# Loading v as nine consecutive tokens per partition, with its quadrants moved on VectorE and the left-over keys of two heads taken together

## The chip, the cores and the metric

The kernel runs on one core of a Trainium2 chip. The time is the device time of one execution in microseconds (us); it is given as the median of several runs. Five engines run side by side, each with its own instruction list in order: TensorE (PE in the profile; PEld is its weight load), VectorE (DVE), ScalarE (ACT), GpSimd (POOL) and SyncE (SP). They wait for one another by semaphores. 16 DMA engines move data between the chip's memory (HBM) and the on-chip memory (SBUF); PE writes its results to PSUM, which DVE and ACT read.

## The reference

Two stages, cut to what matters. First an attention over 8 batches, 8 heads, 576 tokens and 64 channels, with a bias from the running sum of a gate s:

```python
scores = q @ k.T / sqrt(64)
cum = cumsum(max(s, 0))
bias = -(cum[query] - cum[key])
scores = where(key > query, -1e9, scores + min(bias, 0))
x = softmax(scores) @ v                  # [8, 576, 8*64]
```

Then a mixing of the lowest 64 frequencies of x along the tokens, with one complex 512x512 matrix per frequency, and a product with w_ch:

```python
X = rfft(x, axis=tokens)[:64]
Y = X @ (w_r + 1j * w_i)                 # per frequency
u = x + irfft(Y, n=576)
out = u + max(u @ w_ch, 0)               # [8, 576, 512] float32
```

The 64 pairs of matrices are 134 MB in float32; q, k and v are 9.4 MB each.

## The kernel before

**Steps.** The attention goes in 32 steps n. Step n handles batch b = n % 8 of head pair g = n // 8, so both heads of a pair. The order of work is written out by hand: the loop near the end of the attention part calls, in each step, `load` (issues DMAs on POOL), `cum_rows` (the queries' part of the bias, by SP), `scores(n, 0)`, `av(n-1, 1)`, `mode_products(n)`, `transposes(n+1, 0)`, `scores(n, 1)`, `transposes(n+1, 1)`, `fft(n-1)` and `av(n, 0)`. PE, DVE and ACT each run their own instructions in the order of these calls. In steps 26 to 31 two products with w_ch for rows that are already complete are put in: `first_transposed(i, 0)` after `scores(n, 1)`, and `first_product(i, 0)`, `first_transposed(i, 1)`, `first_product(i, 1)` after `av(n, 0)`. `first_transposed` is four transposes on PE and a copy by DVE (xt, L538); `first_product` is four matmuls (z_ps, L546) on that copy.

**q and k** are loaded by `loads_qk` for two steps at once, 18 consecutive tokens per partition, turned by PE (tr_ps, L340) in two halves and copied to qt and kt, three of four copies by DVE and one by ACT (L344).

**Scores.** Keys are taken in two windows of 256 tokens, W = 2*P, and each window in two tiles r of 128 keys: tile r holds the keys 2p + r of partition p. `scores(n, h)` makes, for r = 0 and 1, one PSUM tile `sc_ps` of 1,024 columns from a pool of two buffers (`scpool`): two matmuls that write the causal mask (negm, L376), three that add the scores of both windows (L382), and two exps on ACT that write p_sb in fp16 (L390), 576 and 320 queries wide. The last 64 tokens of the 576 are left over; their keys come from `scores4`, called for both heads together with the second head's first tile: it writes 64 spare columns of that same PSUM tile (L353, L357), for the last 64 queries alone, and one exp makes p4 (L361).

**v** is loaded by `loads_v` in each step, one DMA per head with 2 consecutive tokens per partition (512 bytes in memory, 256 as fp16), straight into the layout that `av` reads (v2, five buffers); the 64 left-over tokens of all batches of a head pair come by `loads_tails` in two DMAs into v4.

**av(n, h)** multiplies p by v for five blocks of 128 queries: 17 matmuls with 65 columns (64 channels and a one, which gives the softmax's sum; L418). The sums of the two tiles r lie in two columns, so DVE adds them (den, L423), inverts (L427) and scales the result into x_all (L428).

**fft and modes.** `fft(n-1)` transforms x_all (L443) and DVE copies the result to xs in four casts (L453). `modes(g, c)` multiplies xs by the weights of eight frequencies (L463); the products for head pair g are made while pair g+1 is in the attention, those of the last pair after step 31.

**Loads.** All loads of q, k, v and weights are issued by POOL (L234) in the order of the lists given to `load`, which spreads the lists over one another; each issue waits for one of eight semaphores taken in turn, so for the DMA eight issues before, and, where a buffer is used again, for its reader. Weights have a ring of 11 and one of 6 buffers and eight early places; the memory types are changed from float32 to 16 bits by the DMA.

**After step 31** come the mode products of the last head pair, one group of eight frequencies after another as their weights arrive, with products with w_ch between them, and then the output, 18 DMAs.

Of the kernel before, what the change touches and what calls it, by code (L numbers as in the profile page):

```python
# [18 lines left out]
def kernel(  # L19
# [11 lines left out]
    nc = tc.nc  # L31
# [23 lines left out]
    W = 2 * P  # L55
    NWN = S // W
    NK = 2 * NWN
    HM = NM // 2
# [3 lines left out]
    ident_np = np.eye(P, dtype=np.float32)  # L62
    negm_np = np.concatenate(
        [np.where(2 * np.arange(P)[:, None] + r > np.arange(W)[None, :], -1.0e9, 0.0) for r in range(2)],
        axis=1,
    )
    nat = np.arange(NL)
    negm4_np = np.concatenate([np.where(nat[:, None] > nat[None, :], -1.0e9, 0.0)] * 2, axis=0)
# [55 lines left out]
    NV = LA + 2  # L124
    VW = 66


    v2 = [ap_.tile([P, 2 * NWN * W + P], FP16, name=f"v2_{i}") for i in range(NV)]

    v4 = [ap_.tile([P, B, VW], FP16, name=f"v4_{i}") for i in range(2)]  # L130
    NP_ = 3
    poff = [0]
    for w in range(NWN):
        for r in range(2):
            poff.append(poff[-1] + SP - w * W)
    p_sb = [ap_.tile([P, poff[-1]], FP16, name=f"p_sb{i}") for i in range(NP_)]
    p4 = [ap_.tile([P, P], FP16, name=f"p4_{i}") for i in range(2)]

    temp = xs_flat[1].bitcast(FP32)
    ident32, negm32, s_sb = temp[:, :P], temp[:, P : P + 2 * W + NL], temp[:NPAIR, -S:]  # L140
    ident16 = ap_.tile([P, P], BF16, name="ident16")
    negm = ap_.tile([P, 2 * W + NL], BF16, name="negm")
# [20 lines left out]

    def loads_v(n):

        if n >= N:
            return []
        g, b = divmod(n, B)
        return [
            (  # L170
                v2[n % NV][:, : 2 * NWN * W].rearrange("p (w h c) -> p w h c", w=NWN, h=2)[:, :, h, P:],
                v[b, 2 * g + h, : NF * P, :].rearrange("(w p r) d -> p w (r d)", p=P, r=2),
            )
            for h in range(2)
        ]

    def loads_tails(g):

        if g >= NG:
            return []  # L180
        return [
            (
                v4[g % 2][NL * h : NL * h + NL, :, :D],
                v[:, 2 * g + h, NF * P :, :].rearrange("b t d -> t b d"),
            )
            for h in range(2)
        ]


# [75 lines left out]
    load(loads_w(W0), loads_v(0) + loads_tails(0) + first[2:] + loads_v(1))  # L265
# [7 lines left out]
    with tc.tile_pool(name="cum_psum", bufs=1, space=PSUM) as cpsum:  # L273
        spos = s_sb
        zer, cum = (p_sb[i][:NPAIR, :].bitcast(FP32)[:, :S] for i in (0, 1))
# [9 lines left out]
        keys = cum[:, : NF * P].rearrange("c (w p r) -> c w r p", p=P, r=2)  # L285
        for x in range(NK):
            nc.tensor.transpose(
                ct_ps[:, x, :], keys[:, x // 2, x % 2, :], ident32[:NPAIR, :NPAIR]
            )

        tl = p_sb[2][:NPAIR, :].bitcast(FP32)[:, : 2 * NL].rearrange("p (x t) -> p x t", x=2)
        for x in range(2):
            nc.vector.tensor_copy(out=tl[:, x, :], in_=cum[:, (NT - 1) * P :])
        nc.tensor.transpose(
            ct_ps[:, NK, :], tl.rearrange("p x t -> p (x t)"), ident32[:NPAIR, :NPAIR]
        )
        nc.vector.tensor_copy(out=cumt_sb, in_=ct_ps)
        for x in range(2):
            rows = slice(NL * x, NL * x + NL)
            nc.vector.tensor_copy(  # L300
                out=cumt4[rows, :], in_=cumt_sb[rows, NK, x::2]
            )
# [4 lines left out]
    for i in range(NV):  # L307
        for c in (P - 1, W):
            nc.vector.memset(
                v2[i][:, c : c + (2 * NWN - 1) * W + 1 : W], 1.0  # L310
            )
    for i in range(2):
        nc.vector.memset(v4[i][:, :, D : D + 1], 1.0)
        nc.vector.memset(p4[i][:, NL * (1 - i) : NL * (2 - i)], float(1 - i))
# [17 lines left out]
    def transposes(n, half):  # L332
# [8 lines left out]
        for i, dst in enumerate((qt, kt)):  # L341
            copy = (nc.vector.tensor_copy, nc.scalar.copy)[half * i]
            to = dst[n % NQ][:D].rearrange("d h (p r) -> d h p r", r=R)
            copy(  # L344
# [629 lines left out]
```

## Time and profile before

| what | value |
|---|---|
| median of 3 runs | 443.83 us (443.63 to 443.93) |
| span of the profiled execution | 441.4 us; the median of the runs is 2.4 us above it |
| busy, share of the span | PE 344.0 us (78%), DVE 253.2 (57%), ACT 226.2 (51%), POOL 241.5 (55%) |
| DMA | 93.25 MB in 72,768 packets, 29,760 of them under 512 B |
| v loads | 72 DMAs of 64 KB, 0.72 us of POOL each |
| weight loads | 256 KB each, median 8.5 to 9.1 us from issue to landing |
| start of step 8, 16, 24, 26, 31 (L357 on PE) | 75.0, 151.1, 243.8, 276.6, 326.6 us |
| first mode product after step 31 | 335.6 us |
| last weights used | 405.4 to 407.5 us |

How to read it: the page cuts the span in 40 slices of 11 us; a digit is the busy share in tenths, for DMA the mean of its 16 engines. A line of a timeline is: start in us, length in us, engine, line of the kernel, operation, what it writes <- what it reads, shape, count; in brackets the idle time of the engine just before it and what ended that. Sizes in GB/s are counted on the written side, so 16-bit data that come from float32 count half of what is read.

### The profile page before, as it was taken

The numbers are of one execution on the slowest core, as the hardware profiler recorded it, in microseconds if no ns is written. First come the engines' busy times: TensorE is split into PE (matmuls) and PEld (weight loads), VectorE is DVE, ScalarE is ACT, GpSimd is POOL, SyncE is SP. The second block draws the span as 40 slices with busy tenths as digits, with TensorE's granted clock in tenths as the row PEclk, the third lists the DMA queues.
The fourth block names the chain that finished last, engine by engine and source line by source line (L and its number), as shares of the span: only waits on it lengthen the run. The fifth ranks groups of instructions, "written<-read, shape, count | busy, mean of one in ns | idle before, by whom it ended". The sixth has DMA issues, their size and how long they took to land.

```text
span 441.4 us, 10806 instructions
## 1 busy us (share of the span) xinstructions
PE 344.0 (78%) x4409; PEld 207.5 (47%) x4409; DVE 253.2 (57%) x574; ACT 226.2 (51%) x421; POOL 241.5 (55%) x381
## 2 busy tenths in 40 slices
PE   1688998898686978792956658989987887787994
PEld 1455656465354545460634325655554445442341
DVE  7766775676545546471643515766655443451795
ACT  1486788267545725571543324666650424420794
POOL 7766566565565655555655555555544444440293
PEclk9998999999969889896786967999998988998999
DMA  9999999999999999999999999999999999998498
GB/s 180 201 206 206 204 206 205 207 207 206 209 199 207 205 208 207 207 207 208 202 206 206 208 207 203 208 205 206 200 209 211 209 210 209 210 213 163 154 383 343
DMA packets 72768, 93.25 MB, mean 211 GB/s; under 512 B 29760, under 2 KB 31296, under 8 KB 72720
## 3 DMA queue, kind: packets, MB, share of 16 engines
q0 software_dynamic: 63408, 81.29, 105.0%
q1 hardware_dynamic: 9312, 11.29, 7.7%
q8 instruction: 34, 0.56, 0.5%
q14 instruction: 14, 0.11, 0.1%
HBM read 163.51 MB, written 9.44 MB: 392 GB/s over the span
## 4 chain that ended last, share of the span: by engine, by line
DMA 53%; PE 24%; DVE 12%; issue 5%; ACT 3%; POOL 2%; DVEq 0%; ACTq 0%; POOLq 0%
DMA w_sb<-in_moe_w_i_dram 31%; DMA w_sb<-in_moe_w_r_dram 20%; PE yp L463 3%; PE sc_ps L382 3%; PE z_ps L655 3%; DMA qk<-in_k_dram 2%; PE u_ps L781 2%; DVE qt L344 2%; PE sc_ps L376 2%; POOL w_sb L234 2%; PE u_ps L751 2%; DVE xs L453 2%; PE av_ps L418 2%; PE tr_ps L340 2%; DVE xt L538 1%
## 5 line engine op out<-in xcount | busy, mean ns | idle before, releaser
L390 ACT ACTIVATE p_sb<-sc_ps,cumt_sb 128x576 f16<-128x576 f32 (+1 forms) x256 | 141.9, 636 | 22.2 <-PE sc_ps L382 21.8
L234 POOL DMA_DIRECT2D w_sb<-in_moe_w_r_dram x120 | 71.1, 594 | 59.1 <-DMA w_sb<-in_moe_w_i_dram 18.1
L234 POOL DMA_DIRECT2D w_sb<-in_moe_w_i_dram x120 | 70.9, 593 | 55.0 <-DMA w_sb<-in_moe_w_i_dram 20.2
L382 PE MATMUL sc_ps<-qt,kt 128*128 128x512 bf16 (+2 forms) x384 | 78.3, 317 | 8.2 <-ACT kt L344 7.5
L344 DVE COPY qt<-tr_ps 64x576 bf16<-64x576 bf16 x64 | 47.8, 746 | 52.5 <-PE tr_ps L340 52.5
L234 POOL DMA_DIRECT2D v<-in_v_dram x72 | 52.0, 722 | 41.3 <-DMA w_sb<-in_moe_w_r_dram 10.7
L340 PE MATMUL tr_ps<-ident,qk 64*64 64x64 bf16 x1152 | 34.6, 205 | 43.9 <-DMA qk<-in_k_dram 15.0
L382 PEld LDWEIGHTS <-kt 128*128 128x128 bf16 x384 | 38.7, 106 | 37.2 <-ACT kt L344 14.7
L340 PEld LDWEIGHTS <-qk 64*64 64x64 bf16 x1152 | 26.5, 117 | 60.7 <-DVE kt L344 19.0
L376 PE MATMUL sc_ps<-negm,ident 128*128 128x256 bf16 x256 | 54.2, 297 | 0.2
L463 PE MATMUL yp<-w_sb,xs 128*32 128x512 bf16 (+1 forms) x480 | 42.0, 415 | 15.2 <-DMA w_sb<-in_moe_w_i_dram 13.6
L361 ACT ACTIVATE p<-sc_ps,cumt 128x64 f16<-128x64 f32 x32 | 10.1, 314 | 78.0 <-PE sc_ps L357 77.8
L418 PE MATMUL av_ps<-v,p_sb 128*128 128x65 f16 x1024 | 44.3, 197 | 1.2 <-DVE x_all L428 0.5
L344 ACT COPY kt<-tr_ps 64x576 bf16<-64x576 bf16 x32 | 22.9, 715 | 37.7 <-DVE qt L344 37.2
L418 PEld LDWEIGHTS <-p_sb 128*128 128x128 f16 x1024 | 37.8, 100 | 8.4 <-DVE x_all L428 3.4
L453 DVE CAST xs<-ft_ps 64x128 bf16<-64x128 f32 x128 | 36.6, 286 | 7.2 <-PE ft_ps L443 5.8
L423 DVE TENSOR_REDUCE den<-av_ps 128x5 f32<-128x10 f32 x64 | 10.8, 169 | 50.3 <-PE av_ps L418 49.3
L463 PEld LDWEIGHTS <-xs 128*32 128x32 bf16 (+1 forms) x512 | 18.9, 145 | 32.2 <-DMA w_sb<-in_moe_w_i_dram 14.0
L428 DVE TENSOR_TENSOR x_all<-av_ps,rcp 128x320 f16<-128x320 f32 x64 | 31.5, 492 | 2.2
L524 ACT COPY z<-z_ps 128x512 f32<-128x512 f32 x22 | 12.9, 586 | 26.7 <-PE z_ps L546 14.1
L443 PE MATMUL ft_ps<-Ff_sb,x_all 128*64 128x192 f16 (+1 forms) x320 | 24.1, 264 | 1.0 <-DVE x_all L428 1.0
L344 DVE COPY kt<-tr_ps 64x576 bf16<-64x576 bf16 x32 | 24.4, 762 | 0.4
(108 smaller groups left out, 432.9 us busy)
## 6 DMA issues: line engine op xcount, KB each, us to landing
w_sb<-in_moe_w_r_dram POOLq DMA_DIRECT2D x120, 256.0 KB, 8.5
w_sb<-in_moe_w_i_dram POOLq DMA_DIRECT2D x117, 256.0 KB, 9.1
out_dram<-r_w SPq DMA_DIRECT2D x16, 512.0 KB, 3.0
v<-in_v_dram POOLq DMA_DIRECT2D x72, 64.0 KB, 7.4
qk<-in_q_dram POOLq DMA_DIRECT2D x15, 288.0 KB, 8.0
qk<-in_k_dram POOLq DMA_DIRECT2D x15, 288.0 KB, 9.1
x_all<-in_moe_w_i_dram POOLq DMA_DIRECT2D x6, 256.0 KB, 7.7
y_acc<-in_moe_w_r_dram POOLq DMA_DIRECT2D x4, 256.0 KB, 7.9
```

Of the source, the lines that this page charges most:

```text
L234: nc.gpsimd.dma_start(out=dst, in_=src)
L340: nc.tensor.transpose(ps[rows, r, :], src[rows, r, :], ident16[rows, rows])
L344: copy(out=to[:, :, :, half * RH : half * RH + RH], in_=ps[HP * i : HP * i + HP].rearrange("d r (h p) -> d h p r", h=2),)
L376: nc.tensor.matmul(ps[:, bass.ds(w * S, W)], ident16, negm[:, bass.ts(r, W)], start=True, stop=False, skip_group_check=True,)
L382: nc.tensor.matmul(ps[:, c0 : c0 + i1 - i0], keys[:, w, r, :], qh[:, i0:i1], start=False, stop=True, skip_group_check=True,)
L390: nc.scalar.activation(out=pt[:, poff[x] : poff[x] + S - w * W], in_=ps[:, w * S : (w + 1) * S - w * W], func=ACTF.Exp, bias=cumt_sb[:, x, ...
L418: nc.tensor.matmul(ps[:, I, r : r + NCH], lhsT, rhs, start=(i == 0), stop=(i == len(todo) - 1), skip_group_check=True,)
L428: nc.vector.tensor_tensor(out=x_all[:, g, b, :, D * h : D * h + D], in0=ps[:, :, 1 : NCH], in1=rcp.unsqueeze(2).to_broadcast([P, NT, D]), ...
L443: nc.tensor.matmul(ps[HP * q_ : HP * q_ + HP].rearrange("p h f -> p (h f)"), x_all[:nT, g, b, T, q_::2], Ff_sb[:nT, T, :], start=(T == 0), ...
L453: nc.vector.tensor_copy(out=xs[g % 2][HP * h : HP * h + HP, q_, :, h, :, b, :], in_=a)
L463: nc.tensor.matmul(ps[32 * cg : 32 * cg + 32, :], cols[k0:, q_, 1 - ri, :, c * MC // 2 + cg], wt[(g, c, ri, cg // 2)][k0:, 2 * (cg % 2) + ...
L655: nc.tensor.matmul(zs[i, x], xts[i][:, x, dt, :], wch_sb[:, dt, :], start=(dt == 0), stop=(last and dt == DT - 1), skip_group_check=True,)
```

## The change

- **Blocks of 288 keys.** W becomes 32*9 = 288, so two windows cover all 576 keys. A partition of the loaded v holds 9 consecutive tokens; 8 of them make two key tiles c of 128 keys (4 tokens from each of 32 partitions), the ninth is left over: 32 keys per window and head. kt is written in that order, so that a tile is 128 neighbouring columns.
- **v.** One DMA per two steps brings both heads' v of two batches, 9 tokens per partition (2,304 bytes in memory, 1,152 as fp16), into a buffer vf; the tails' loads go. `place_v` moves it on DVE into the layout that `av` reads: 16 copies per two steps, each of 32 partitions to another group of 32 partitions, and one of 128 partitions for the ninth tokens (v4). `place(n)` calls half of them in each step, after `av(n, 0)` (in steps 8, 16 and 24 at the end).
- **Left-over keys.** `scores4` takes a PSUM tile of its own from `scpool`, between the second head's two tiles: two mask matmuls and six of 32 rows by 288 queries, and an exp over 576 queries. `av` gets five more matmuls per head for them and loses the one of before.
- **The sum.** All products of a block go to the same 65 columns, so the addition den goes.

The two versions' instruction lists differ in count as follows: PE matmuls 4,406 before and 4,822 after, DVE copies by `place_v` 0 and 272, den 64 and 0, load DMAs by POOL 363 and 308; ACT 420 and 420. In the changed list the first matmul of the second head's second score tile waits for ACT.

The core of the diff:

```diff
-    W = 2 * P
+    RV = RH
+    W = RP * RV
...
+    vpool = at.enter_context(tc.tile_pool(name="v_sb", bufs=3))
...
-    v2 = [ap_.tile([P, 2 * NWN * W + P], FP16, name=f"v2_{i}") for i in range(NV)]
+    v2 = [ap_.tile([P, 2, 2 * NWN, 2, VW], FP16, name=f"v2_{i}") for i in range(2)]
...
     def loads_v(n):
...
+        t = fat[n // 2] = vpool.tile([P, 2, RV * D], FP16, name="vf", tag="vf")
         return [
             (
-                v2[n % NV][:, : 2 * NWN * W].rearrange("p (w h c) -> p w h c", w=NWN, h=2)[:, :, h, P:],
-                v[b, 2 * g + h, : NF * P, :].rearrange("(w p r) d -> p w (r d)", p=P, r=2),
-            )
-            for h in range(2)
+                t[:, x0:x1],
+                v[b + x0 : b + x1, 2 * g : 2 * g + 2].rearrange("b h (p r) d -> (h p) b (r d)", r=RV),
+            )
+            for x0, x1 in ([(0, 2)] if n else [(0, 1), (1, 2)])
         ]
...
+    def place_v(n, h):
+
+        if n >= N:
+            return
+        f, to = fat[n // 2], v2[n // 2 % 2]
+        for i in range(2 * h, 2 * h + 2):
+            rows = f[RP * i : RP * i + RP, :, : 8 * D].rearrange("p b (c j d) -> p b c j d", c=2, j=4)
+            for j in range(4):
+                nc.vector.tensor_copy(out=to[RP * j : RP * j + RP, :, i, :, :D], in_=rows[:, :, :, j])
+        if h == 0:
+            nc.vector.tensor_copy(out=v4[n // 2 % 2][:, :, :D], in_=f[:, :, 8 * D :])
...
-    def scores4(n, ps):
+    def scores4(n):
...
+        ps = scpool.tile([P, 1024], FP32, name="sc_ps", tag="sc")
+        cols = [ps[:, 512 * w : 512 * w + W] for w in range(NWN)]
...
+        for wq_ in range(NWN):
+            for wk in range(wq_ + 1):
+                for h in range(2):
+                    r0 = HP * h + RP * wk
+                    nc.tensor.matmul(
+                        cols[wq_][r0 : r0 + RP], kt[n % NQ][:, h, wk * W + 2 * P : (wk + 1) * W],
+                        qt[n % NQ][:, h, wq_ * W : (wq_ + 1) * W],
+                        start=False, stop=True, tile_position=(0, r0), skip_group_check=True,
+                    )
...
-        for r in range(2):
+        for c in range(2):
+            if h == 1 and c == 1:
+                scores4(n)
             ps = scpool.tile([P, 1024], FP32, name="sc_ps", tag="sc")
...
-            if h == 1 and r == 0:
-                scores4(n, ps[:, 2 * S - W : 2 * S - W + NL])
...
+            todo.append((I, p4[n % 2][rows, t0 : t0 + P], v4[n // 2 % 2][rows, n % 2, :NCH]))
...
-        den = rpool.tile([P, NT], FP32, name="den", tag="den")
-        nc.vector.tensor_reduce(
-            out=den, in_=ps[:, :, 0 : VW : NCH], axis=mybir.AxisListType.X, op=ALU.add
-        )
...
+    def place(n):
+
+        if n % 2:
+            place_v(n + 1, 0)
+        else:
+            place_v(n, 1)
...
-            load((loads_qk(n + LA) if n % 2 else []) + loads_v(n + LA) + tails_due, loads_w(on_chip[n]))
+            load(loads_qk(n + LA) + loads_v(n + LA) if n % 2 else [], loads_w(on_chip[n]))
...
+            if n == 0:
+                place_v(0, 0)
             fft(n - 1)
             av(n, 0)
+            place(n)
             if i is not None:
                 first_product(i, 0)
                 first_transposed(i, 1)
```

## The prediction

> **What bounds the kernel now.** I read the page's slices first.
>
> ```profile
> span 441.4 us, 10806 instructions
> ...
> DMA  9999999999999999999999999999999999998498
> GB/s 180 201 206 206 204 206 205 207 207 206 209 199 207 205 208 207 207 207 208 202 206 206 208 207 203 208 205 206 200 209 211 209 210 209 210 213 163 154 383 343
> ```
>
> The DMA engines never rest until about 405 us: 206 GB/s while v is being loaded, 210 once only weights are left. So up to there a transfer limit is at work, and the end comes 36 us later. But the chain of waits passes from 264 to 325 us through PE and DVE, not through DMA, so I listed PE's idle time over the whole span. PE last waits for a qk load at 235.6 us and for weights at 250.6, 261.3, 264.1 and 274.9 (1.3, 1.6, 2.4 and 1.0 us); after that only here:
>
> ```profile
> 352.31 0.43 PE L463 MATMUL yp<-w_sb,xs 128*32 128x512 bf16 x2 [1.01 <-DMA w_sb<-in_moe_w_i_dram]
> 354.82 1.07 PE L463 MATMUL yp<-w_sb,xs 128*32 128x512 bf16 x6 [2.07 <-DMA w_sb<-in_moe_w_i_dram]
> ...
> 405.42 0.65 PE L463 MATMUL yp<-w_sb,xs 128*32 128x512 bf16 x4 [0.70 <-DMA w_sb<-in_moe_w_i_dram]
> ```
>
> So two chains run side by side and almost touch: the load stream, and, from 275 us on, a computing chain with only 1.01+2.07+0.70 = 3.8 us of waiting left in it. Before 275 us computing waits for loads (some 37 us from step 12 on) and has room. From 275 us on it has almost none: steps 26 to 31, about 10.2 us each, then the mode products of the last head group. **Any delay in steps 26 to 31 beyond what the loads give back moves the end.**
>
> **Part 1: fewer, longer v packets.** I compared the DMA view of a stretch with v loads (50 to 60 us) and of one with weights only (320 to 380 us):
>
> ```profile
> DMA packets 2477, 2.03 MB, mean 203 GB/s; under 512 B 1639, under 2 KB 1639, under 8 KB 2474
> ```
>
> ```profile
> DMA packets 7013, 12.58 MB, mean 210 GB/s; under 512 B 912, under 2 KB 912, under 8 KB 7008
> ```
>
> The second takes 60/12.58 = 4.77 us per MB. At that price 2.03 MB need 9.68 us, so 0.32 us went to about 1,490 extra small packets: 0.21 ns each. A straight line through all 39 ten-microsecond windows from 10 to 400 us gives 0.27 ns, which I use. Today v makes 64 x 256 + 8 x 512 = 20,480 packets; afterwards 4,096 of 1,152 B each. 55 fewer DMAs also save about 16 completion packets each, 880 (912 small packets stand beside 48 weight DMAs above). That is 17,300 to 21,400 packets, 4.7 to 5.8 us over the whole stream; 28 of the 32 steps' v is through by step 26, so the stream is 4.1 to 5.1 us early there.
>
> From this 0 to 3 us are given back early. Step 0 gets two sets of copies (4 us, part 2), the prologue one more copy of the running sums (about 0.75, the row of the 64x576 TENSOR_SCALAR beside it); with 0.3 us per step after that (part 2) step 8 comes some 7 us late. Its products free the first ring buffers, and POOL already waits 2.87 us there (issue at 85.7 us). A load takes 8.5 to 10 us from issue to landing, so the queue covers about that much: 2.9+7+1 = 11 us is 1 more than it covers. **Lead at step 26: 3.5 us** (1 to 5).
>
> A rule that would make more of it: the Trainium skill, "DMA: Bandwidth & Descriptors", section "Bandwidth", measures a lone 64 KB transfer at 138 GB/s and calls transfers below that descriptor-dominated. By it the 4.7 MB of v take 34 us instead of 22, an estimate of 12 us saved. The trace has such loads among others at 203 GB/s, and the trace decides.
>
> **Part 2: steps 26 to 31.** One late step on PE, ACT and DVE, from three timeline views:
>
> ```profile
> 306.38 0.22 PE L357 MATMUL sc_ps<-qt,kt 128*64 128x64 bf16 x2
> 306.53 0.39 PE L376 MATMUL sc_ps<-negm,ident 128*128 128x256 bf16 x2
> 306.76 0.55 PE L382 MATMUL sc_ps<-qt,kt 128*128 128x512 bf16 x3
> 307.14 0.39 PE L533 MATMUL xt_ps<-ident16h,x_all 128*128 128x128 f16 x4
> ...
> 311.62 1.04 PE L546 MATMUL z_ps<-wch_sb,xt 128*128 128x512 f16 x4 [1.00 <-DVE xt L538]
> ```
>
> ```profile
> 306.88 2.20 ACT L390 ACTIVATE p_sb<-sc_ps,cumt_sb 128x576 f16<-128x576 f32 x4
> ```
>
> ```profile
> 306.76 0.76 DVE L344 COPY kt<-tr_ps 64x576 bf16<-64x576 bf16 x1
> 307.56 0.69 DVE L538 CAST xt<-xt_ps 128x512 f16<-128x512 f32 x1
> ...
> 308.83 1.19 DVE L453 CAST xs<-ft_ps 64x128 bf16<-64x128 f32 x4
> ...
> 310.48 0.49 DVE L428 TENSOR_TENSOR x_all<-av_ps,rcp 128x320 f16<-128x320 f32 x1
> 310.89 0.68 DVE L538 CAST xt<-xt_ps 128x512 f16<-128x512 f32 x1
> 314.52 0.17 DVE L423 TENSOR_REDUCE den<-av_ps 128x5 f32<-128x10 f32 x1 [2.96 <-PE av_ps L418]
> ```
>
> DVE works without a gap from 306.0 to 311.6; PE waits for its last copy (xt) and then makes DVE wait 2.96 us. In such a ring, work added in the busy half is not hidden by the idle half.
>
> (a) *A new wait.* scores4 leaves the spare columns of a score tile and takes one of the two buffers of the pool `sc` for itself, between the second head's two tiles. So the second of these needs the buffer of the first, and PE must wait for its two exps (the changed instruction list has this wait on ScalarE). ACT does four exps in 2.20 us, so 1.10 for two. First tile ready near 306.6 (0.2 us later than now, from part c), exps until about 307.8, second tile 0.61 us long (306.53 to 307.14 now), so xt_ps starts at 308.44 instead of 307.14. DVE, done with kt at 307.5, starts xt at 308.87 instead of 307.56: 1.31 us late. The removed reduce gives back 0.2. **+1.1 us, six times.** Queued behind the waiting matmul on PE are the transposes, fft and av(n,0).
>
> (b) *The copies.* place(n) puts eight 32 x 256 fp16 copies between x_all (310.48) and xt (310.89), in steps 26 to 30. No such row exists. Below: a 128x4 memset is 62 ns, eight are 0.5 us. Above: the 128-element xs cast is 286 ns, and from 512 elements (686) to 576 (746) a copy grows 0.94 ns per element, so 256 cost 0.41, eight 3.3 us. Nearest are the two casts from SBUF to SBUF, L303 (128 elements, 227 ns) and L304 (576, 454 ns): 0.51 ns per element, 292 ns for 256; fp16 sources may do better, and the fixed part alone is 162. I take 0.25 us, and no overlap between neighbours, since the four xs casts, which also change partition half, take 1.19 us at 286 ns each. **+2.0 us, five times** (0.5 to 3.3); one v4 copy in steps 27 and 29, 0.25 each.
>
> On the overlap the skill has a rule against the change: "VectorE: DVE Perf Modes", section "Two Vector instructions with no wait between them", says that an instruction whose output starts in another 32-partition group than the last one is held until that has finished. Here x_all to xt overlap by 0.08 us (310.48+0.49 against 310.89); by such overlap the eight would cost 1.4, by the rule 2.0.
>
> (c) *PE.* av has 21 matmuls per head instead of 17 (17 take 0.72 us, 303.50 to 304.22, so 42 ns each: +0.17); scores have 32 columns more per tile (+0.01); scores4 about 0.55 instead of 0.27. In the late ring 0.2 of this counts per step and stands in (a). Only the last av adds 0.2 more. ACT: exp of p4 0.65 instead of 0.21, four others 0.03 shorter: +0.3 us, inside ACT's idle 1.3 us per step.
>
> Sum for steps 26 to 31: 6 x 1.11 + 5 x 2.0 + 2 x 0.25 + 0.2 = **17.4 us**.
>
> In the other steps (example 47.5 to 54.1, 6.62 long) DVE waits 0.57 and 0.89 us for PE, and two reduces of 0.21 go: 1.67 of 2.0 us of copies is covered, 0.3 us is left; were the copies 3.3 us, 1.6. From step 12 on the waits for loads cover it. If vf lands after DVE reaches its copies, all of DVE queues behind them; v is issued two or three loads after k, about 4 us, while the copies come some 4 us after the transposes that need k, so I cost that at nothing up to 1 us, inside the same slack. The 52 us that POOL spends issuing v shrink to a quarter: nothing, POOL waits for DMA anyway.
>
> **Sum.** 17.4 - 3.5 (lead) - 3.8 (waits for weights that vanish, as the weights are then in time) = +10.1 us. Nothing after step 31 is edited. The profiled span 441.4 becomes 451.5; the median of the runs, 443.83, lies 2.4 above the span, so **453.9 us**.
>
> **Rivals.** (1) *Faster:* the load stream alone sets the end. If the step's waits overlapped so that steps 26 to 31 grew less than 3.5+3.8 = 7.3 us in all (1.2 per step), the end would be the stream's: 443.8 - 4.3 = 439.5. For it: DMA busy until 405 us. Against: the 1.00 us that PE waits for xt in every late step, and 1.1 of new wait alone makes 6.7. (2) *Half:* copies at 0.11 us, 0.9 per step: 17.4 - 5.5 = 11.9, lead 3.5: 448.4. (3) *Worse:* copies at one element per cycle, 3.3 us: steps grow by 23.9, early steps by 1.6 each, so step 8 is 17 us late, loads stop there and the lead is gone: 443.8 + 23.9 - 3.8 = 463.9, or 462.2 if half of the lead stays. (4) *The packets don't shrink, or cost no more than their bytes:* lead 0, 457.4; the changed load has 1,152 B rows, so this is a part of the forecast's range.
>
> **Chances.** Forecast with (4), 449 to 459: 0.52. (2), 444.8 to 449: 0.18. (3), above 459: 0.15. (1), under 442.9: 0.12. Within 0.2%, about what a measurement here can tell from no change: 0.03. Faster 0.12, same 0.03, slower 0.85. The range, 445 to 461, leaves out (1), the same, and the far end of (3).
>
> **What would show it.** Right: a wait of PE at the second score tile of head two for ACT of about 1 us in every step; xt copies 2 us after x_all in steps 26 to 30; late steps of 13.3 us; waits at 352 to 355 gone; GB/s 2 to 4 higher before 300 us. Wrong: late steps under 11.5 us, waits of yp for weights still there after the last attention step, or copies of 0.1 us.

## The result and the profile after

| | median, us | range, us | runs |
|---|---|---|---|
| before, beside it | 443.88 | 443.63 to 443.95 | 4 |
| after | 498.96 | 497.37 to 501.47 | 4 |

The ratio is 1.125 (95% interval 1.122 to 1.127): the changed kernel is 55 us slower. The prediction was 453.9, with a range up to 461: the direction was right, the size was not.

From the page of the changed kernel: span, busy time of PE and DVE, then the DMA engines' share and rate in 40 slices (12.5 us each), and the packets.

```profile
span 498.2 us, 11723 instructions
...
PE 409.4 (82%) x4766; PEld 248.7 (50%) x4825; DVE 306.5 (62%) x775; ACT 242.4 (49%) x421; POOL 201.7 (40%) x326
...
DMA  8999999939999998899999999999876799996396
GB/s 188 213 210 163 202 172 175 198 63 184 180 202 166 207 208 157 136 205 210 209 210 209 211 208 210 209 209 184 144 133 106 138 202 207 209 169 130 135 383 263
DMA packets 55511, 93.62 MB, mean 188 GB/s; under 512 B 8401, under 2 KB 14033, under 8 KB 55457
```

The packets fell by 17,257 as meant, and where the loads run freely they run at about 210 GB/s. But they no longer run all the time: 63 GB/s in slice 8, 106 in slice 30 (slices are counted from 0 here and below). The chain of waits of the changed kernel has changed sides. Before it was DMA 53%, PE 24%; now, by engine and by line:

```profile
PE 69%; DVE 15%; ACT 9%; issue 3%; DMA 2%; DVEq 0%; ACTq 0%
PE av_ps L433 21%; PE sc_ps L399 9%; PE sc_ps L393 8%; PE yp L474 8%; ACT p_sb L405 7%; DVE v L191 6%; PE tr_ps L345 5%; PE z_ps L676 4%; PE ft_ps L454 4%; DMA qt<-ncum_sb 2%; PE u_ps L802 2%; DVE x_all L439 2%; PE u_ps L772 2%; PE z_ps L772 1%; PE z_ps L557 1%
```

A fifth of that chain is `av`, whose added matmuls the prediction had given 0.17 us per head. So I looked at one head's `av` on PE. First before (the third row is what follows, so its start is the end of `av`):

```profile
303.50 0.66 PE L418 MATMUL av_ps<-v,p_sb 128*128 128x65 f16 x16
304.09 0.20 PE L418 MATMUL av_ps<-v,p 64*128 64x65 f16 x1
304.22 0.44 PE L463 MATMUL yp<-w_sb,xs 128*32 128x512 bf16 x4
```

Then after:

```profile
56.92 0.24 PE L433 MATMUL av_ps<-v,p_sb 128*128 128x65 f16 x2
57.09 0.20 PE L433 MATMUL av_ps<-v,p 64*128 64x65 f16 x1
57.22 0.30 PE L433 MATMUL av_ps<-v,p_sb 128*128 128x65 f16 x4
57.45 0.20 PE L433 MATMUL av_ps<-v,p 64*128 64x65 f16 x1
57.59 0.30 PE L433 MATMUL av_ps<-v,p_sb 128*128 128x65 f16 x4
...
58.49 0.20 PE L433 MATMUL av_ps<-v,p 64*128 64x65 f16 x1
58.62 0.42 PE L393 MATMUL sc_ps<-negm,ident 128*128 128x288 bf16 x2
```

Read the starts, not the lengths. Before, 16 products over 128 rows need 0.59 us (37 ns each) and `av` is through in 0.72. After, a group of four needs 0.23 us where 4 x 37 ns make 0.15, and each product over 64 rows (p4 and v4) 0.13: five of these stand between the others, and `av` takes 1.70 us. That is 1 us more per head, 2 us per step.

The late step, first PE: the two waits that the prediction named are there.

```profile
308.73 0.41 PE L393 MATMUL sc_ps<-negm,ident 128*128 128x288 bf16 x2 [0.68 <-ACT p_sb L405]
...
315.92 1.04 PE L557 MATMUL z_ps<-wch_sb,xt 128*128 128x512 f16 x4 [2.25 <-DVE xt L549]
```

And DVE ahead of the second of them: x_all, the eight copies in 1.89 us, xt.

```profile
312.75 0.49 DVE L439 TENSOR_TENSOR x_all<-av_ps,rcp 128x320 f16<-128x320 f32 x1
313.25 1.89 DVE L191 COPY v<-vf 32x256 f16<-32x256 f16 x8
315.18 0.69 DVE L549 CAST xt<-xt_ps 128x512 f16<-128x512 f32 x1
```

PE waits nowhere for weights after the last attention step. It is the other way round: over the span, POOL, which issues the loads, waits for PE to free buffers. Longest waits of POOL, total us, times, longest:

```profile
POOL w_sb L238 <- PE yp L474: 88.8, 13, 15.6
POOL qk L238 <- PE tr_ps L345: 55.9, 9, 8.5
```

### The profile page after: what moved, and what is told of

Read it like the earlier page. It is cut to its first block, busy times and chain, and to the rows that moved or that the text cites. A ratio compares the mean times of both kernels' runs of the same rounds, so it can differ in the third digit from the quotient of the medians.

```text
span 498.2 us, 11723 instructions
## 1 busy us (share of the span) xinstructions
PE 409.4 (82%) x4766; PEld 248.7 (50%) x4825; DVE 306.5 (62%) x775; ACT 242.4 (49%) x421; POOL 201.7 (40%) x326
## 4 chain that ended last, share of the span: by engine, by line
PE 69%; DVE 15%; ACT 9%; issue 3%; DMA 2%; DVEq 0%; ACTq 0%
PE av_ps L433 21%; PE sc_ps L399 9%; PE sc_ps L393 8%; PE yp L474 8%; ACT p_sb L405 7%; DVE v L191 6%; PE tr_ps L345 5%; PE z_ps L676 4%; PE ft_ps L454 4%; DMA qt<-ncum_sb 2%; PE u_ps L802 2%; DVE x_all L439 2%; PE u_ps L772 2%; PE z_ps L772 1%; PE z_ps L557 1%
## 5 line engine op out<-in xcount | busy, mean ns | idle before, releaser
L433 PE MATMUL av_ps<-v,p_sb 128*128 128x65 f16 x1024 | 91.1, 201 | 8.6 <-DVE v L191 8.5
L393 PE MATMUL sc_ps<-negm,ident 128*128 128x288 bf16 x256 | 57.6, 310 | 19.4 <-ACT p_sb L405 19.4
L399 PE MATMUL sc_ps<-qt,kt 128*128 128x64 bf16 (+2 forms) x325 | 61.2, 291 | 10.9 <-ACT kt L355 4.6
L433 PEld LDWEIGHTS <-p_sb 128*128 128x128 f16 x1024 | 52.8, 100 | 27.1 <-issue 6.4
L433 PE MATMUL av_ps<-v,p 64*128 64x65 f16 x320 | 64.8, 203 | 1.2 <-DVE v L193 1.2
L191 DVE COPY v<-vf 32x256 f16<-32x256 f16 x256 | 60.9, 238 | 3.5
L438 DVE RECIPROCAL rcp<-av_ps 128x5 f32<-128x5 f32 x64 | 12.4, 194 | 62.6 <-PE av_ps L433 62.6
L464 DVE CAST xs<-ft_ps 64x128 bf16<-64x128 f32 x128 | 36.7, 287 | 10.3 <-PE ft_ps L454 9.0
L433 PEld LDWEIGHTS <-p 64*128 64x128 f16 x320 | 29.7, 93 | 18.4
L393 PEld LDWEIGHTS <-ident 128*128 128x128 bf16 x256 | 20.8, 100 | 33.2 <-issue 27.4
L238 POOL DMA_DIRECT2D qk<-in_q_dram x17 | 10.1, 595 | 60.7 <-PE tr_ps L345 55.9
```

Source lines behind the costliest of these rows:

```text
L191: nc.vector.tensor_copy(out=to[RP * j : RP * j + RP, :, i, :, :D], in_=rows[:, :, :, j])
L238: nc.gpsimd.dma_start(out=dst, in_=src)
L393: nc.tensor.matmul(ps[:, bass.ds(w * S, W)], ident16, negm[:, bass.ts(c, W)], start=True, stop=False, skip_group_check=True,)
L399: nc.tensor.matmul(ps[:, c0 : c0 + i1 - i0], kt[n % NQ][:, h, bass.ds(w * W + c * P, P)], qh[:, i0:i1], start=False, stop=True, skip_group ...
L433: nc.tensor.matmul(ps[:, I, :NCH], lhsT, rhs, start=(i == 0), stop=(i == len(todo) - 1), skip_group_check=True,)
L464: nc.vector.tensor_copy(out=xs[g % 2][HP * h : HP * h + HP, q_, :, h, :, b, :], in_=a)
```

## The experiments

The theory after the first look: **each change between weights of 128 and of 64 rows costs PE about 0.1 us** (nine changes inside a head's `av`, and the cover that the early steps were to give is not there). Rivals: the 64-row product itself is slow wherever it stands; or neither, the number of products or another tile costs. Besides, the loads, the copies and the new wait had to be priced one by one.

All times in one table. "Step 8" is how much later than before the first head's x_all of step 8 starts on DVE. "Loads lost" is worked out from each page: the shortfall of GB/s under 210 in slices 2 to 10 of the page's 40, counted from 0, in us. "Steps 26 to 31" is from x_all of step 25 to x_all of step 31, first head.

| kernel | median, us | ratio to before, 95% | step 8, us later | loads lost, us | steps 26 to 31, us |
|---|---|---|---|---|---|
| before | 443.8 | | 0 | 1.8 | 58.4 |
| after | 499.0 | 1.122 to 1.127 | 28.4 | 20.3 | 84.9 |
| e1 tail last | 469.5 | 1.056 to 1.060 | 19.1 | 9.4 | 82.7 |
| e2 wide tail | 470.7 | 1.058 to 1.065 | 19.4 | 9.7 | 82.0 |
| e3 = e1, scores4 first | 468.0 | 1.051 to 1.058 | 16.3 | 6.7 | 84.4 |
| e5 = e1, late copies later | 454.7 | 1.023 to 1.031 | 17.6 | 7.9 | 68.2 |
| e6 = e3 and e5 | 452.2 | 1.016 to 1.023 | 21.5 | 11.4 | 63.8 |
| e9 = e6, early copies earlier | 454.5 | 1.023 to 1.026 | 21.6 | 11.7 | 62.8 |
| e10 = e1, no copies | 445.0 | 0.999 to 1.005 | 6.1 | 0.3 | 67.7 |
| e11 = e6, four copies on ACT | 444.7 | 1.0005 to 1.0055 | 10.3 | 0.9 | 62.6 |
| e12 = e11, early copies earlier | 445.4 | 1.001 to 1.006 | 13.8 | 4.4 | 64.6 |
| e13 = e11, tail in between | 466.8 | 1.048 to 1.057 | 19.1 | 10.1 | 75.3 |
| e4 = before, new loads alone | 441.8 | 0.995 to 0.997 | 0.9 | 0.3 | 60.0 |
| e8 = before, tail in the middle | 443.7 | 0.999 to 1.001 | 1.3 | 1.7 | 58.7 |

### The switches of rows

**e1: the 64-row products behind the others.**

```diff
             todo.append((I, p4[n % 2][rows, t0 : t0 + P], v4[n // 2 % 2][rows, n % 2, :NCH]))
+        todo.sort(key=lambda m: m[1].shape[0], reverse=True)
```

> The changed kernel with one edit: in av, the five 64-row products of p4 and v4 stand behind the sixteen 128-row ones instead of one after each group of them. Nothing else moves. In the changed kernel one av takes about 1.65 us from its first matmul to its last (300.61 to 302.31), where 17 took 0.72 us before. Theory 1, every switch of PE between 128-row and 64-row operands costs time (about 0.1 us each, nine of them per head): only one switch is left, av takes about 0.9 us, the 64 heads win some 45 us together, and the total falls to about 454 us (450 to 460), which is my forecast with its step on PE as I had put it. Theory 2, a 64-row product is slow wherever it stands (0.13 us): av takes about 1.25 us and the total is about 480. Theory 3, neither; it is the number of products or their data: av stays at 1.65 and the total at 499.

469.5 us, 29.5 less. One head's `av` in its timeline, with what follows:

```profile
300.60 0.68 PE L434 MATMUL av_ps<-v,p_sb 128*128 128x65 f16 x16
301.21 0.32 PE L434 MATMUL av_ps<-v,p 64*128 64x65 f16 x5
301.46 0.82 PE L558 MATMUL z_ps<-wch_sb,xt 128*128 128x512 f16 x3
```

The same 21 products take 0.86 us instead of 1.70, and five 64-row products in a row take 0.25: they are not slow. The second and third theory fall. But the total stops at 469.5, not at 454: the switches are not the whole miss.

**e2: the order kept, all products of 128 rows**, v4 once per head with zeros in the other head's rows.

```diff
-    v4 = [ap_.tile([P, 2, VW], FP16, name=f"v4_{i}") for i in range(2)]
+    v4 = [ap_.tile([P, 2, 2, VW], FP16, name=f"v4_{i}") for i in range(2)]
...
-            todo.append((I, p4[n % 2][rows, t0 : t0 + P], v4[n // 2 % 2][rows, n % 2, :NCH]))
+            todo.append((I, p4[n % 2][:, t0 : t0 + P], v4[n // 2 % 2][:, n % 2, h, :NCH]))
```

> The changed kernel with the order of av's products kept, but all of them of 128 rows: v4 is held once per head with zeros in the rows of the other head, so that each p4 product takes all 128 rows of p4. It costs one more v4 copy on VectorE in every second step (0.25 us). Theory 1 (the switch of rows costs) and theory 2 (64-row products are slow) both give av of about 0.9 us and a total of about 454 us (450 to 460). Theory 3 (the number of products, or another tile in between, costs): av stays at 1.65 us and the total at 499. Beside the run with the tail last, this tells theory 1 from theory 2: if both runs come to 454, it is the switch; if only this one does, it is the 64-row product.

470.7 us, as e1. In its timeline the products of p4 now stand between the others at no price (0.03 us from start to start, and 0.13 for four):

```profile
309.40 0.19 PE L437 MATMUL av_ps<-v,p 128*128 128x65 f16 x1
309.43 0.29 PE L437 MATMUL av_ps<-v,p_sb 128*128 128x65 f16 x4
309.56 0.19 PE L437 MATMUL av_ps<-v,p 128*128 128x65 f16 x1
```

Same order, same number, other row count: the switch is what costs.

**e8: one more switch in the kernel before.**

```diff
-        todo.append((NT - 1 - b % 2, 1, p4[n % 2][rows, :], v4[g % 2][rows, b, :NCH]))
+        todo.insert(len(todo) // 2, (NT - 1 - b % 2, 1, p4[n % 2][rows, :], v4[g % 2][rows, b, :NCH]))
```

> The kernel before with one edit: the single 64-row product of av's left-over keys stands in the middle of the sixteen 128-row ones instead of behind them, so that PE has one more switch of rows per head and nothing else is changed. Theory 1 (switches cost about 0.1 us): av takes 0.8 to 0.9 us instead of 0.72 in the trace; in the twelve heads of the late steps, where the computing chain sets the end, 0.1 to 0.2 us per step stand on the path, so the total is 0.5 to 1.5 us above before, 444.5 to 445.5. Theories 2 and 3: av and the total unchanged, 0.72 us and 443.8.

```profile
304.02 0.41 PE L418 MATMUL av_ps<-v,p_sb 128*128 128x65 f16 x8
304.36 0.20 PE L418 MATMUL av_ps<-v,p 64*128 64x65 f16 x1
304.49 0.42 PE L418 MATMUL av_ps<-v,p_sb 128*128 128x65 f16 x8
```

From the first start to the last end `av` takes 0.89 us here against 0.79 before: 0.10 us for one switch, without anything of the change. Eight more switches at 0.10 and four more products at 37 ns make 0.95, the step from 0.72 to 1.70 (0.98). The total did not move (443.7), below the 0.5 to 1.5 us I had expected: steps 26 to 31 grow by 0.3 us in the table, where twelve switches make 1.2, so most of one switch per head is hidden there.

**e13: the switches put back into the best version** (e11, below); its diff to e11 is e1's added line taken out.

> The best kernel so far (444.7 us: tail last, scores4 first, late copies behind the second xt, four of the even steps' early copies on ScalarE) with the 64-row products put back between the 128-row ones, as the change has them. This prices the switches by themselves, where the copies cost nothing. Each av takes 0.84 us more (1.77 against 0.93, from the first start to the last end). If the switches are a term of their own, on the path in the late steps (two heads, 1.7 us per step, six steps: 10 us) and in the early ones through loads that stop (steps 0 to 8, 15 us later, of which the queue of loads covers what it covered for the others, some 8 to 10): 444.7 + 10 + 5 to 10 = 460 to 465 us. If they only hurt together with the copies (PE and VectorE in one ring): under 455. If they are worth what their removal won in the changed kernel, 29.5 us, here too: 474.

466.8 us, 22.1 more than e11: a little above the case of an own term (460 to 465), far from "only together" (under 455), and under the 29.5 that their removal won in the changed kernel. Steps 26 to 31 grow by 12.7 us and the early loads lose 9.2 more; together 21.9.

The Trainium skill has the rule that would have warned me: "TensorEngine Tiling (Array Packing)", section "Tiling Modes", says that a change of tiling mode, unlike one of tile alone, drains the TensorEngine. These runs show a price, not the drain itself: 0.10 us per change for products of 65 columns.

### The loads

**e4: the new loads of v in the kernel before**, no copies, a constant in place of v.

```diff
-                v2[n % NV][:, : 2 * NWN * W].rearrange("p (w h c) -> p w h c", w=NWN, h=2)[:, :, h, P:],
-                v[b, 2 * g + h, : NF * P, :].rearrange("(w p r) d -> p w (r d)", p=P, r=2),
+                t[:, x0:x1],
+                v[b + x0 : b + x1, 2 * g : 2 * g + 2].rearrange("b h (p r) d -> (h p) b (r d)", r=RH),
```

> The kernel before with the changed loads of v alone: nine tokens per partition, one load for two heads and two batches, no loads of left-over keys. The copies between quadrants are left out, and the products read a constant instead of v, so the values of v do not reach the output. Keys, scores and products have the sizes and the order of before. My part 1: the stream of loads is 4.7 to 5.8 us shorter, and the end comes 3.8 to 4.7 us earlier (the waits of the mode products for weights), 439 to 440 us. Rival, packets cost no more than their bytes: the same time as before, 443.8 us. A third possibility, that POOL's issuing of v held the stream back as well: under 438 us.

441.8 us, 2.0 less, about half of what I expected. Its slices on the page:

```profile
GB/s 179 211 209 211 209 209 209 209 210 209 210 209 209 209 210 209 208 210 209 209 210 209 210 209 206 209 210 209 210 209 210 210 209 209 211 216 95 235 398 239
```

About 210 throughout (206 to 211 in slices 1 to 34) instead of 199 to 209 while v is loaded, x_all of step 26 3.7 us earlier and of step 31 3.6 (the lead that the prediction put at 3.5), the last y transposes on PE 4.5 us earlier (404.17 against 408.65). Up to there the estimate of 4.3 holds. Then 2.8 us are lost at the end: from the start of DVE's last pair of sums to the end of the span there are 5.5 us before (435.93 to 441.4), 8.3 here (431.46 to 439.8), and as many in the changed kernel (489.95 to 498.2). No computing stands in that gap, but rows of the program's closing line do (shortest, median and longest in ns, then the first and the last start in us). Before:

```profile
L969 POOLq DRAIN  x3: 45/102/3705, 432.6 to 441.1; - x3
L969 SPq DRAIN  x3: 7/7/7, 440.6 to 440.9; - x3
```

And in e4:

```profile
L963 POOLq DRAIN  x3: 45/102/10880, 428.1 to 439.5; - x3
L963 POOLq EVENT_SEMAPHORE  x4: 17/17/17, 439.0 to 439.7; - x4
L963 SPq DRAIN  x3: 7/7/7, 436.1 to 439.2; - x3
```

The longest DRAIN of POOL is its first: 3.7 us before, 10.9 us here and in every other kernel with the new loads. It ends at 439.0, 2.9 us after SP has seen the output land (436.1), and only then do the engines close together; before, it ended at 436.3 and SP came last (440.6). Why the DRAIN is longer stays open.

### The copies and the clock

**e10: e1 without any copy**; the products read a constant, so v's values are left out.

```diff
     def place_v(n, h):
+        return
...
-        nc.vector.memset(v2[i][:, :, :, :, D], 1.0)
+        nc.vector.memset(v2[i], 0.5)
```

> The kernel with the tail last (469.5 us) without any of the copies between quadrants: the products read a constant, so the values of v do not reach the output; all loads, scores and products stay. By my forecast only steps (a) and (c) and the loads are left: 443.8 + 6 x 1.1 + 0.2 - 3.5 - 3.8 = 443.3 us, and the early steps are back near 6.9 us. The copies would then be worth 26 us of the 469.5, not the 11 that I gave them: 11 as I had put it for the late steps, and the rest from the lowered clock behind PE's longer waits and from the early steps. Rival: the early steps stay at 7.2 to 10 us without the copies, because of PE (scores4, more products): about 455 us.

445.0 us, 1.7 above the 443.3 that is left of the prediction without its term (b). The copies cost 24.5 us in e1; I had given them 10.5. (The products of e10 wait for no load of v either, but that is not what went: DVE stood idle 3.5 us in all ahead of e1's 256 copies.) The early steps are 7.2 us each, as with the wait of 0.68 us for ACT alone.

**e5: e1 with the late copies behind the second xt cast.**

```diff
             av(n, 0)
-            place(n)
+            if i is None:
+                place(n)
             if i is not None:
                 first_product(i, 0)
                 first_transposed(i, 1)
+                place(n)
```

> The kernel with the tail last (469.5 us) with one edit: in steps 26 to 31 the eight copies of v run on VectorE behind the second xt cast instead of ahead of it, where VectorE waits 3 to 5 us for PE. Theory, the copies are on the ring and, by the idle of 2.74 to 2.90 us that they make on PE, the granted TensorE clock falls (0.68 in the window 320 to 330 us): five steps win 1.9 us each for the copies, and those with a lowered clock some 2 us more (four of five): 469.5 - 9.5 - 8 = 452 us. If the copies count but the lowered clock does not matter: 460. Rival, the lost time of the late steps is not the copies (the ring is set by PE and the new wait for ACT): 468 to 470.

454.7 us, 14.8 less, for five sets of copies of 1.9 us. So more than the copies went. What went with them is seen in e1's own timeline of PE: the wait for xt, with the copies ahead of it, is 2.90 us long, and the rows behind it are 1.6 times as long as usual until 326.1 (av 1.09 against 0.68, the mask 0.69 against 0.42):

```profile
320.63 1.89 PE L558 MATMUL z_ps<-wch_sb,xt 128*128 128x512 f16 x4 [2.90 <-DVE xt L550]
322.31 0.69 PE L393 MATMUL sc_ps<-negm,ident 128*128 128x288 bf16 x2
...
324.71 1.09 PE L434 MATMUL av_ps<-v,p_sb 128*128 128x65 f16 x16
...
327.62 0.42 PE L393 MATMUL sc_ps<-negm,ident 128*128 128x288 bf16 x2
```

The windows of e1 from that wait on give the granted clock (the number ahead of the DMA share): half speed throughout the first 5.5 us.

```profile
320.60:326.10 5.50, 5.47 (x35) 3.12 (x35) 0.00 (x0) 2.80 (x5) 0.00 (x0) 0.50 0.95 178
326.10:331.60 5.50, 4.82 (x86) 3.02 (x84) 3.72 (x7) 2.85 (x6) 4.44 (x8) 0.97 0.80 107
```

The clock fell to half, for 3.4 or 6.8 us, behind four of e1's five waits of 2.7 to 2.9 us, behind two of five of 2.9 to 3.2 in e2, and behind two of five of 2.2 to 2.5 in the changed kernel. What a fall costs is seen where a kernel has steps of both kinds: e2's three middle late steps take 13.2 and 13.5 us without one and 15.1 with one, the changed kernel's 14.4 and 14.4 against 15.8. Which waits are hit goes with their place: the clock changes on a grid of 3.41 us (e1's four falls start at 292.2, 305.9, 319.5 and 336.6, which are 4, 4 and 5 times 3.41 apart), and in the 3.41 us ahead of them PE is busy 0.65, 0.63, 1.60 and 0.67 us. The idle time of the fifth wait is split over two such stretches, and the clock stays. Here are the one ahead of the fourth fall and the two of the fifth wait (PE's busy time stands behind the length of 3.41):

```profile
333.19:336.60 3.41, 0.67 (x7) 0.37 (x6) 3.13 (x12) 0.58 (x1) 0.00 (x0) 1.00 1.13 204
...
346.83:350.24 3.41, 1.94 (x29) 1.18 (x25) 3.23 (x13) 1.50 (x3) 0.05 (x1) 1.00 1.14 215
350.24:353.65 3.41, 2.10 (x14) 1.25 (x15) 1.20 (x4) 0.94 (x2) 0.00 (x0) 1.00 1.12 207
```

In e5 the copies stand where DVE waits for PE anyway:

```profile
321.38 2.00 DVE L191 COPY v<-vf 32x256 f16<-32x256 f16 x8
323.39 0.20 DVE L193 COPY v<-vf 128x128 f16<-128x128 f16 x1
324.58 0.20 DVE L439 RECIPROCAL rcp<-av_ps 128x5 f32<-128x5 f32 x1 [0.99 <-PE av_ps L434]
```

After 2.2 us of copies DVE still waits 0.99, the clock is 1.00 in all windows from 290 to 340 us, and a late step takes 11.3 us instead of 14 to 16. The Trainium skill, "TensorE: Matmul & The Clock Gate", section "What's actually happening", gives half speed after an idle window of some 3.4 us, and says that these windows run freely and do not begin anew with a kernel. The grid of 3.41 us agrees with that; but the rows show the drop after gaps of 2.2 to 3.2 us too, shorter than that window, and after stretches in which PE was not idle throughout.

**e3: scores4 ahead of head two's first tile** (in e1).

```diff
-            if h == 1 and c == 1:
+            if h == 1 and c == 0:
                 scores4(n)
```

> The kernel with the tail last (469.5 us) with one edit: scores4 runs ahead of head two's first score tile instead of between its two tiles. In that kernel PE waits 0.68 us per step at head two's second tile for the two exps of its first (19.4 us in 32 waits). Theory: the wait is on the path wherever PE or the ring of PE and DVE sets the step; then the second tile waits for one exp of p4 (0.74 us) instead of two (1.13), some 0.3 to 0.4 us less per step, in 20 to 32 steps: 457 to 463 us. Rival: the wait only moves, or its time is given back at the wait for xt or for loads: 468 to 470 us.

468.0 us, 1.5 less, with intervals that just meet (1.056 to 1.060 for e1, 1.051 to 1.058 here). The theory's 457 to 463 was wrong. The wait is nearly gone (2.8 us in 18 waits up to 260 us, 14.5 in 24 in e1), but in the late steps PE only comes earlier to the wait for xt (15.0 us in all, 14.9 in e1), and in the early steps to the wait for copies, below.

**e6: both.** Its diffs are those of e3 and e5.

> The kernel with the tail last with both edits: scores4 ahead of head two's first tile, and the late copies behind the second xt cast. If the two are independent, the sum of what each wins by itself: 469.5 - 8 - 17 = 444 us (441 to 450). If both remove the same wait of the ring, no more than the larger of the two alone, about 452.

452.2 us: the sum of what the two won by themselves (1.5 and 14.8 make 453.2), not of what I had expected of each. Against e5 it is 2.5 us, with intervals that meet. Late steps are down to 10.9 us, against 10.2 before. Much of the loss that is left lies before step 10: e6's loads lose 11.4 us there.

### The early steps

Why are they late? In e1, in the odd steps, PE waits for the copies themselves: `place(n)` of an even step moves the second head's v, which `av(n, 1)`, half a step on, needs.

```profile
65.75 0.36 PE L434 MATMUL av_ps<-v,p_sb 128*128 128x65 f16 x6 [1.25 <-DVE v L191]
66.81 0.61 PE L434 MATMUL av_ps<-v,p_sb 128*128 128x65 f16 x10 [0.70 <-DVE v L191]
```

**e9: e6 with these copies at the start of the even step.**

```diff
             av(n - 1, 1)
+            if n and n % 2 == 0 and n < N - len(first_pairs):
+                place_v(n, 1)
```

> The kernel with both edits and a third: in the even steps up to 24 the eight copies for the second batch row of a pair run at the start of the step, ahead of everything else on VectorE, instead of behind av, where av of the next head waits for them (1.25 and 0.70 us in the step at 65.75 us; 16.1 us in 20 waits in the kernel with the tail last). Theory: these waits made the early steps late (odd steps 9 to 10.5 us against 6.6 before), so that step 8 freed the weight buffers late and the loads stopped at 105 GB/s in slice 8; with them gone the total falls by 3 to 8 us under the kernel with both edits. Rival: the copies then delay the transposes' copies by as much: the same time as the kernel with both edits.

454.5 us, 2.3 above e6 with intervals that just meet: the rival was right. PE's longest wait in total is now the one for kt, behind the copies on DVE:

```profile
PE tr_ps L345 <- DVE kt L355: 29.0, 12, 4.4
```

**e11: e6 with four of the even steps' eight early copies on ACT**, at their old place.

```diff
-                nc.vector.tensor_copy(out=to[RP * j : RP * j + RP, :, i, :, :D], in_=rows[:, :, :, j])
+                copy = nc.scalar.copy if i in act else nc.vector.tensor_copy
+                copy(out=to[RP * j : RP * j + RP, :, i, :, :D], in_=rows[:, :, :, j])
...
-            place_v(n, 1)
+            place_v(n, 1, (2,) if 0 < n < N - len(first_pairs) else ())
```

> The kernel with both edits (scores4 first, late copies behind the second xt; 452.2 us) with four of the eight copies of the even steps up to 24 given to ScalarE, at the same place. Theory: in the early steps VectorE is the bound (two steps hold about 14.2 us of its work, 4.4 of them copies), PE waits for its copies at the next av (17.1 us in 20 waits), and late early steps stop the loads (120 GB/s in slice 9): with 1 us less on VectorE in every second step the waits fall by about 1 us each, and the total by 2 to 4 us: 448 to 450. Rival: ScalarE's copies stand behind its exps of the scores and come later than VectorE's: same or slower, 452 to 456.

444.7 us, 7.5 less than e6 and more than expected, although a copy on ACT takes 402 ns against 236 on DVE. Two steps (4 and 5) shrink from 18.8 to 15.0 us, step 8 is 10.3 us late instead of 21.5, and the slices of e11 show the loads going on:

```profile
GB/s 187 212 210 209 207 209 209 209 201 209 209 209 210 209 210 209 209 210 209 209 209 209 209 209 209 209 210 208 210 210 209 210 209 210 209 218 111 231 395 244
```

**e12: e11 with the even steps' copies behind the first half of the transposes.** In its diff `place(n)` moves from behind `av(n, 0)` to behind `transposes(n + 1, 0)`, in even steps up to 24.

> The kernel before it, with the even steps' copies (four on VectorE, four on ScalarE) right behind the first half of the transposes instead of behind av. Theory: av of the next head no longer waits for them, and one microsecond each on two engines fits beside the scores: early steps of 7.2 us on average, loads that do not stop, 443 to 447 us. Rival: the second half of the transposes then waits for VectorE, as where all eight copies stood at the start of the step (PE waited 29.0 us for kt there): 450 to 455.

445.4 us, the same as e11 within the intervals. The waits are exchanged: up to 260 us PE waits 3.2 us for copies on DVE instead of 9.4 on DVE and ACT, and 9.3 us for the exp of p4 instead of 2.5.

## Why the prediction was right in sign and wrong in size

Without the copies and the switches the prediction's own terms make 443.3 us; e10 measured 445.0. The copies were put at 10.5 and cost 24.5 (e1 less e10); the switches were put at nothing and cost 29.5 (after less e1). 445.0 + 24.5 + 29.5 = 499.0: of the 45.1 us that were missed, 29.5 stem from the switches, 14.0 from the copies, 1.7 from the rest. The split holds for things taken away in this order; put back into e11, where the copies cost little, the switches took 22.1.

By place, most of it came early: x_all of step 25 is 30.9 us late, where the forecast had it 3.5 us early, and steps 26 to 31 add 26.5, where it had 17.4. Without copies and switches (e10) x_all of step 25 is 4.2 us early.

- **Step (c), the step that failed.** "av has 21 matmuls per head instead of 17 (17 take 0.72 us, 303.50 to 304.22, so 42 ns each: +0.17)". The mean of 17 rows of one kind was taken for a product of another kind at another place. It was +0.98 per head. The trace of before did hold the clue: the one 64-row product behind sixteen others took 0.13 us (304.09 to 304.22) where the others took 37 ns each; and the diff puts such a product behind each block. I divided 0.72 by 17 and averaged the clue away. The rivals held no such case.
- **The early steps, "0.3 us is left" and "From step 12 on the waits for loads cover it": wrong.** They take 8.9 and 11.1 us in turn instead of 6.6; 7.2 without copies and switches. The 0.68 us wait of (a) was counted in six late steps only, and stood in all 32 (19.4 us). And that DVE's waits for PE would cover 1.67 of 2.0 us of copies left out that PE waits for the same copies: `av(n, 1)` needs what `place(n)` has just moved.
- **The queue of loads: right, with wrong input.** "So the queue covers about that much", which was 10 us. In the table, loads lost are step 8's lateness less 9 to 10 us in nine of the ten kernels where step 8 is over 10 us late, and 8.1 in the changed kernel, where more is lost later. The prediction put step 8 at 7 us late, so 1 us lost; it was 28.4, and 20.3 lost. From there POOL waits for PE, and the cover for computing, the 37 us of waits for loads from step 12 on, is used up, as computing itself is late.
- **Step (a): right in place and, as a sum, in size.** The wait is 0.68 us per step at the named matmul, and with no copies and no switches a middle late step takes 11.34 us (e10, from xt to xt) against 10.20 before: 1.14 more, 1.1 predicted. Taking the wait away gives back 0.42 of it (10.92 in e6) and won 1.5 to 2.5 us in all, hardly more than the runs can tell.
- **Step (b): right in itself.** 238 ns a copy (0.25 predicted), eight in 1.8 to 2.4 us, no overlap, as the rule on neighbouring Vector instructions had it; xt 2.4 us after x_all starts. But behind the wait that it made on PE, 2.2 to 2.9 us, the clock fell, which the prediction did not consider. By subtraction that cost e1 about 5 of the 14.8 us that moving the copies won (14.8 less five times 1.9); no run changed the clock alone, but four falls at the 1.4 to 1.9 us that one costs in e2 and in the changed kernel make 6 to 8, the same order.
- **Late steps: predicted 13.3, measured about 14.7** from xt to xt (13.4 to 16.4 by x_all). With the switches away they take 13.9 to 15.9 in e1, where the clock fell in each of the four measured; where it did not fall, e2's middle ones take 13.2 and 13.5, as forecast. The switches alone make 1.67 per step (12.59 in e13, 10.92 in e11).
- **Part 1: right.** 17,257 packets less, lead 3.7 us at step 26 in e4, saturated slices at 209 to 210. The 12 us that the rule on 64 KB transfers would have made of it are far off. The end won only 2.0 of 4.3 us, as POOL's longer DRAIN costs 2.8 us at the close, a term that the prediction did not have. In the changed kernel nothing of the lead is left: the waits for weights after the attention (3.8 us) did go, but because PE's first mode product came 59 us later (394.4 us against 335.6 before).
- **Rivals.** "Worse" (459 to 464) had the right picture, loads that stop early and no lead, but for copies at 3.3 us a set; the copies had the forecast's 2.0 and there were the switches on top. "Faster, the load stream alone" (439.5) is what e4 comes near to: 441.8.

No version that gives the reference's output beats the kernel before: the best, e11, is 0.05 to 0.55% slower. The new loads are worth 2 us, and with the copies and tails placed well the rest of the change still costs about 3.

## What to carry to other kernels

Price an instruction by a row of its own shape and in its own neighbourhood, not by the mean of a group: a matmul over 64 rows among matmuls over 128 costs two switches of 0.1 us, so put such products together or pad them with zeros. Before calling work hidden in an engine's idle time, look at who needs its result next; the same copies cost 24.5 us in e1 and, moved and in part given to ACT, some 2 in e11 (444.7, against 445.0 for e10, which has no copies but lacks the 1.5 to 2.5 us of e3's edit). A stream of loads with a fixed ring of buffers forgives lateness up to what the queue holds, here 10 us, and passes on every microsecond beyond that.

## What the runs showed of the hardware

- A switch of PE between weights of 128 and of 64 rows costs 0.10 us; the 64-row products themselves are not slower (five in a row 0.25 us with one switch in it).
- The granted clock fell to 0.50, for 3.4 or 6.8 us, behind waits of PE of 2.2 to 3.2 us, though not behind every one of them: eight of fifteen in three kernels (after, e1, e2). The length of one wait does not decide it: in the kernel before it is 0.50 from 337.8 to 341.2 us, behind two waits of 1.0 us.
- A copy of 32 x 256 fp16 elements into another group of 32 partitions takes 0.24 us on DVE and 0.40 on ACT.
- With the loads of v in the new form, POOL's closing DRAIN takes 10.9 us instead of 3.7, and the span ends 8.3 us after the start of the last sums on DVE instead of 5.5. Why the DRAIN is longer is not explained.
